# A recurrent scan with a gated feed-forward on one core: parameters transposed behind the dummies, statistics of slab 2 moved from VectorE to ScalarE, and one y moved a gate step

## The chip, the core and the metric

One core of one Trainium2 chip. The metric is the device time of one launch in microseconds (us). Most executions of a kernel agree within 0.3%, and some lie 1 to 2 us higher. TensorE is called PE here, GpSimd is POOL and the DMA-issuing queue is SP, as in the profile.

## The reference, cut to what matters

```python
xn = layernorm(x)                                   # x: 2048 x 512, bf16
Lam_bar = exp(dt * Lam);  Bu = einsum(xn, B_bar)    # complex state of 512
h_t = Lam_bar * h_{t-1} + Bu_t                      # 2048 steps
s = 2 * real(einsum(h, C)) + xn * Dskip
g = silu((gelu(xn @ w_gate) * (xn @ w_up)) @ w_down)   # F = 1376
return x + s * g
```

## The kernel before

The 2048 tokens are worked through in four slabs of 512. For each slab PE computes 11 gate steps (`gate` and `up`, eight matmuls a step), the inputs u of the scan for the slab that follows, the down projection f, and the outputs y of the slab before, four tiles of eight matmuls. VectorE does the complex recurrence in three pieces (rotate, scan, rotate back into `hst`), the products of gate and up, and the epilogue. ScalarE empties PSUM with Gelu, Silu and copies. It also writes a "seed", the skip term, into the PSUM bank of each y before its matmuls accumulate on it. The kernel has eight PSUM buffers of 512 fp32 columns (`bufs=8`), and a gate step takes two of them.

Engines work in program order. Only VectorE's order is computed at build time: `later` puts work in a queue with an estimated cost, and `dve` lets out what fits before a given time.

```python
# the order of a gate step in slab s > 0
if s > 0 and j in Y_AT[s]:
    y_seed(s - 1, Y_AT[s].index(j))          # ScalarE writes the seed
ffn(s, j, ats[s])                            # PE gate, up; ScalarE Gelu, copy; VectorE product
...
    if j in Y_AT[s]:                         # PE: the eight matmuls of y; VectorE: epilogue
        m = Y_AT[s].index(j)
        epi(s - 1, m, y_mm(s - 1, m, hsts[s - 1], y_pss[s - 1, m]), g2s[s - 1, m])
    if s < NS - 1 and XN_AT[s] <= j < XN_AT[s] + M:
        ln_out(s + 1, j - XN_AT[s])          # scale x of the next slab, transpose it by DMA
...
def ln_act(s, m):                            # statistics on ScalarE (before: slab 3 only)
    for i, f in enumerate((AF.Copy, AF.Square)):
        ACT(out=junk[:], in_=x_tok[:, s * M + m, :], func=f, accum_out=sx[:, s, i, m : m + 1])
# end of slab 1: last y of slab 0, and the load of slab 3 behind its output on SP
        if s > 0 and NFT in Y_AT[s]:
            epi(s - 1, M - 1, ...)
        if s == 1:
            load_x(3)
```

Of the kernel before, what the change touches and what calls it, by code (L numbers as in the profile page):

```python
# [19 lines left out]
def kernel(  # L20
# [129 lines left out]
    def dummies(n):  # L150
        w_ps = psum.tile([P, TS], FP32, name="w_ps", tag="ps")
        for _ in range(n):
            nc.tensor.matmul(w_ps[:, :], lhsT=warm[:, 0:P], rhs=warm[:], start=True, stop=True)
# [5 lines left out]
    def bn(s, m):  # L159
        nc.vector.bn_stats(out=st[:, s, m, :], in_=x_tok[:, s * M + m, :])  # L160

    def bn_end(s, m):
        nc.vector.bn_aggr(out=mv[:, s, m, :], in_=st[:, s, m, :])
# [27 lines left out]
    ch = consts.tile(W3, BF16, name="ch")  # L191


    dummies(6)
    pt_ps = psum.tile([P, 16], BF16, name="pt_ps", tag="ps")
    nc.tensor.transpose(pt_ps[:, :], pv[:, :], ident[0:16, 0:16])
    dummies(4)
    def xnT_out(eng, m, tp, k0=0, k1=KT):
        o = xnT[:, k0:k1, m * P : (m + 1) * P]
        if eng is nc.scalar:  # L200
# [1 line left out]
        else:  # L202
            eng.tensor_copy(out=o, in_=tp[:, k0:k1, :])

    ACT(out=pf[:], in_=pt_ps[:, :], func=AF.Copy)
    nc.gpsimd.tensor_tensor(out=dt_[:], in0=euler[:], in1=ldt, op=ALU.pow)
    GT, GS = nc.gpsimd.tensor_tensor, nc.gpsimd.tensor_scalar
# [4 lines left out]
    GT(out=ang[:], in0=ang[:], in1=kr[:], op=ALU.subtract)  # L212
    GT(out=a1[:], in0=lre, in1=dt_[:], op=ALU.mult)
    GT(out=rho[:], in0=euler[:], in1=a1[:], op=ALU.pow)
    for m in range(2):
        bn(0, m)
    bn_end(0, 0)
    bn_end(0, 1)
    rstd0(0, 2)
    xs = [norm0(0), norm0(1)]  # L220
    tps = [t_xn0(0, xs[0]), t_xn0(1, xs[1])]
    xnT_out(nc.vector, 0, tps[0])
# [2 lines left out]
    bn(0, 3)  # L225
    bn_end(0, 2)
    bn_end(0, 3)
    ACT(out=kr[:], in_=ang[:], func=AF.Abs)
    rstd0(2, 4)
    ACT(out=tiny[:], in_=halfpi[:], func=AF.Sin)  # L230
    xs += [norm0(2), norm0(3)]
# [29 lines left out]
        early[3, up] = gu_mm(0, 3, up, 0, TS // 2)  # L261
    xnT_out(nc.vector, 2, tp2[:, 0, :, :])
    ACT(out=sh[:], in_=ang[:], func=AF.Sin, scale=TWO_PI)
    ACT(out=ch[:], in_=kr[:], func=AF.Sin, scale=-TWO_PI, bias=halfpi[:])
    xnT_out(nc.scalar, 3, tp2[:, 1, :, :])


    s2, c2 = (consts.tile([P, NPT, 2], FP32, name=n) for n in ("s2", "c2"))
# [92 lines left out]
    def later(ready, cost, f, key=None):  # L361
        waiting.append((ready, cost, f, key))
# [3 lines left out]
    U_BUFS = 3  # L366
    Z_BUFS = 9
    U0_AT = (5, 7)
    Y_AT = {1: (8, 9, 10, 11), 2: (3, 4, 5, 6), 3: (2, 4, 6, 8)}
    XN_AT = {1: 1, 2: 3}  # L370

    def u_pair(s, h):
        cols = slice(s * TS, (s + 1) * TS)
# [17 lines left out]
    def rotate(dst, src, h, ops, ready, key):  # L391
        hs = slice(h * H2, (h + 1) * H2)
        W = [P, 2, H2, TS]
        box = {}

        def mul(key, tab):
            def f():
                box[key] = work.tile(W, BF16, name=key, tag=key, bufs=1)
                TT(out=box[key][:], in0=src()[:], in1=tab[:, hs, :].unsqueeze(1).to_broadcast(W), op=ALU.mult)  # L399
            return f  # L400

        def comb(i, op):
            return lambda: TT(out=dst()[i], in0=box["pp"][:, i, :, :], in1=box["qq"][:, 1 - i, :, :], op=op)  # L403

        later(ready, 1.17, mul("pp", cos_b), key)
        later(ready, 1.19, mul("qq", sin_b), key)
        for i in range(2):
            later(ready, 0.62, comb(i, ops[i]), key)
# [50 lines left out]
    def ffn(s, j, at):  # L459
        fs = min(P, F - j * P)  # L460
        if s == 0 and j < SPLIT:
            g_ps, u_ps = (gu_mm(s, j, up, TS // 2, TS, early[j, up]) for up in range(2))
        else:
            g_ps, u_ps = gu_mm(s, j, 0), gu_mm(s, j, 1)
        pe_takes(2 * KT)
        i = j % 2
        if i == 0:
            pair["g"] = work.tile([P, 2, TS], BF16, name="gt", tag="gt", bufs=3)
            pair["u"] = work.tile([P, 2, TS], BF16, name="ub", tag="ub", bufs=3)
        gt, ub = pair["g"], pair["u"]  # L470
        ACT(out=gt[:fs, i, :], in_=g_ps[:fs, :], func=AF.Gelu_apprx_tanh)  # L471
        ACT(out=ub[:fs, i, :], in_=u_ps[:fs, :], func=AF.Copy)  # L472
        lag = 1.4
        if s == 0:
            clk["act"] = max(clk["act"], now() - 0.5) + 1.0
            lag = clk["act"] + 0.4 - now()
        if j == NFT - 1:
            dve(now() + lag, 0.36, lambda: TT(out=at[:fs, j, :], in0=gt[:fs, 0, :], in1=ub[:fs, 0, :], op=ALU.mult))  # L478
        elif i:
            dve(now() + lag, 0.63, lambda: TT(out=at[:, j - 1 : j + 1, :], in0=gt[:], in1=ub[:], op=ALU.mult))  # L480

    def down(s, m, at):
        m0 = m * P
# [70 lines left out]
    def ln_small(s):  # L554
        total, var = sx[:, s, 0, :], sx[:, s, 1, :]

        def f():
            STT(out=mq[:, s, :], in0=total, scalar=-1.0 / (D * D), in1=total, op0=ALU.mult, op1=ALU.mult)
            TSC(out=nm[:, s, :], in0=total, scalar1=-1.0 / D, scalar2=None, op0=ALU.mult)
            STT(out=var, in0=var, scalar=1.0 / D, in1=mq[:, s, :], op0=ALU.mult, op1=ALU.add)  # L560
            TSC(out=var, in0=var, scalar1=EPS, scalar2=None, op0=ALU.add)

        dve(now() + 1.0, 0.3, f)
        nc.gpsimd.tensor_tensor(out=rs[:, s, :], in0=var, in1=mhalf[:], op=ALU.pow)
        nc.gpsimd.tensor_tensor(out=nb[:, s, :], in0=nm[:, s, :], in1=rs[:, s, :], op=ALU.mult)


    zs, y_pss = {}, {}
# [10 lines left out]
    def ln_out(s, m):  # L579
        flush(("z", s - 1, m))  # L580
        xn = work.tile([P, D], BF16, name="xn", tag="xn", bufs=4)
        ACT(out=xn[:], in_=x_tok[:, s * M + m, :], func=AF.Identity, scale=rs[:, s, m : m + 1], bias=nb[:, s, m : m + 1])
        xn_out(s, m, xn)

    def xn_out(s, m, xn):
# [19 lines left out]
    def ln_vector_small(x):  # L605
        G.tensor_scalar(out=vx[:, x, :], in0=mv[:, x, :, 1], scalar1=EPS, scalar2=None, op0=ALU.add)
        G.tensor_tensor(out=rs[:, x, :], in0=vx[:, x, :], in1=mhalf[:], op=ALU.pow)
        G.tensor_tensor(out=nb[:, x, :], in0=mv[:, x, :, 0], in1=rs[:, x, :], op=ALU.mult)
        G.tensor_scalar(out=nb[:, x, :], in0=nb[:, x, :], scalar1=-1.0, scalar2=None, op0=ALU.mult)

    vx = consts.tile([P, NS, M], FP32, name="vx")
    ln_vector(1)
    ln_vector_small(1)
    later(13.0, 1.25, lambda: TT(out=v4(t2_[:]), in0=v4(sa[:]), in1=sB, op=ALU.mult))
    for m in range(M):
        skip(0, m, xs[m])
    xs1 = {}
# [12 lines left out]
    for s in range(NS):  # L630
        for j in range(NFT):
            if s > 0 and j in Y_AT[s]:
                y_seed(s - 1, Y_AT[s].index(j))
            ffn(s, j, ats[s])
            if s == 0:
                if j == 1:
                    coefficients()
                if j in U0_AT:
                    chain(0, U0_AT.index(j), u_pair(0, U0_AT.index(j)), hst0)
                if j == 5:  # L640
                    for m in range(M):
                        later(0.0, 0.72, lambda m=m: (bn(2, m), bn_end(2, m)), "n")
                if j == NFT - 1:
                    flush("n")
                    ln_vector_small(2)
                if j == 8:
                    coefficients_end()
                if 3 <= j < 3 + M:
                    flush(("xn", j - 3))
                    xn_out(1, j - 3, xs1[j - 3])  # L650
                if j == 2 + M:
                    load_c(0)
                    nc.sync.dma_start(
                        out=wd[:, 0 : NFT - 1, :],
                        in_=B_w_down[0 : (NFT - 1) * P, :].rearrange("(k p) d -> p k d", p=P),
                    )
                    nc.sync.dma_start(out=wd[:FL, NFT - 1, :], in_=B_w_down[(NFT - 1) * P : F, :])
                    load_c(1)
            else:
                if j in Y_AT[s]:  # L660
                    m = Y_AT[s].index(j)
                    epi(s - 1, m, y_mm(s - 1, m, hsts[s - 1], y_pss[s - 1, m]), g2s[s - 1, m])
                if s < NS - 1 and XN_AT[s] <= j < XN_AT[s] + M:
                    ln_out(s + 1, j - XN_AT[s])
        if s < NS - 1:
            hsts[s + 1] = work.tile([P, 2, NPT, TS], BF16, name="hst", tag="hst")
            ats[s + 1] = work.tile([P, NFT, TS], BF16, name="at", tag="at")
            for h in range(2):
                chain(s + 1, h, u_pair(s + 1, h), hsts[s + 1])
                if h == 0 and s > 0 and NFT in Y_AT[s]:  # L670
                    y_seed(s - 1, M - 1)
            if s > 0 and NFT in Y_AT[s]:
                epi(s - 1, M - 1, y_mm(s - 1, M - 1, hsts[s - 1], y_pss[s - 1, M - 1]), g2s[s - 1, M - 1])
            if s == 1:
                load_x(3)
            for m in range(M):
                g2s[s, m] = down(s, m, ats[s])
                if s == 0:
                    fold_c(m)
                if s == 1:  # L680
                    ln_act(3, m)
            if s == 1:
                ln_small(3)
# [42 lines left out]
```

## Time and profile before

| | before |
|---|---|
| median of 4 runs | 185.35 us (185.21 to 185.49) |
| profiled span | 183.7 us |
| PE / VectorE / ScalarE / POOL busy | 96% / 87% / 64% / 15% |
| first matmul of slab 1 / 2 / 3 | 51.48 / 93.80 / 137.41 us |
| first matmul of the last, halved y | 178.23 us |

The start times of the slabs are the rulers of this document: PE is nearly always busy, so a wait added or removed shows as a shift of the next slab's start. The prediction shows the page's first row, PE's waits and the timeline, and reads them.

### The profile page before, as it was taken

The page shows a single profiled execution, that of the slowest core. Times are in us where ns is not written, and L with a number is a line of the kernel's source. Part 1 is how long each engine was busy: PE and PEld are TensorE (multiplying, and loading weights), DVE is VectorE, ACT ScalarE, POOL GpSimd, SP SyncE. Part 2 cuts the span into 40 slices and gives each one's busy share as a digit, 9 for nine tenths or more (in the row PEclk, how much of TensorE's full clock was granted, in tenths as well). Part 3 has the DMA queues.
Part 4 walks back from the last instruction along what each step waited for, and adds up shares of the span by engine and source line. Part 5 has one row for each costly group of instructions (what it writes and reads, how often), then busy time and mean ns, then how long its engine had stood idle before and what let it go on. Part 6 is the DMA issues. An engine that isn't in the chain of part 4 may idle for free.

```text
span 183.7 us, 2426 instructions
## 1 busy us (share of the span) xinstructions
PE 175.4 (96%) x840; PEld 84.1 (46%) x855; DVE 160.4 (87%) x251; ACT 116.9 (64%) x207; POOL 27.2 (15%) x50
## 2 busy tenths in 40 slices
PE   6989999999999999999999799999999999999992
PEld 1676444444444444444444344444444444444451
DVE  3579999899999899899958999999999999996063
ACT  3299766768789974474499875667529445574510
POOL 3879917000700000000004000000000000000000
PEclk9999999999999999999999999999999999999999
DMA  5999595790001300100400023300000000000012
GB/s 148 311 362 150 109 235 105 207 249 0 0 0 29 79 10 29 42 15 29 114 4 0 0 57 86 87 5 0 0 0 0 0 30 32 29 29 0 0 48 66
DMA packets 25643, 12.37 MB, mean 67 GB/s; under 512 B 15808, under 2 KB 25632, under 8 KB 25632
## 3 DMA queue, kind: packets, MB, share of 16 engines
q1 hardware_dynamic: 25456, 12.16, 27.7%
q8 instruction: 6, 0.10, 0.2%
q10 hardware_dynamic: 176, 0.07, 0.1%
q14 instruction: 5, 0.04, 0.1%
HBM read 6.46 MB, written 2.10 MB: 47 GB/s over the span
## 4 chain that ended last, share of the span: by engine, by line
PE 73%; DVE 9%; ACT 8%; DMA 3%; issue 2%; POOL 2%; ACTq 1%; SPq 0%; DVEq 0%; POOLq 0%
PE up_ps L243 17%; PE g_ps L243 17%; PE f_ps L487 14%; PE y_ps L507 13%; PE u_ps L382 11%; DVE Ft L429 3%; ACT junk L552 2%; DMA x_tok<-in_A_x_dram 2%; DVE yg L520 2%; DMA pv<-in_A_Dskip_dram 1%; DVE pp L399 1%; ACT gt L471 1%; ACT ub L472 1%; ACT g L492 1%; DVE ot L521 1%
## 5 line engine op out<-in xcount | busy, mean ns | idle before, releaser
L243 PE MATMUL up_ps<-xnT,wu 128*128 128x512 bf16 (+2 forms) x188 | 45.2, 361 | 0.9 <-ACT xnT L201 0.7
L243 PE MATMUL g_ps<-xnT,wg 128*128 128x512 bf16 (+3 forms) x193 | 45.5, 357 | 0.4 <-ACT xnT L201 0.2
L487 PE MATMUL f_ps<-wd,at 128*128 128x512 bf16 (+1 forms) x172 | 38.7, 379 | 0.3
L471 ACT ACTIVATE gt<-g_ps 128x512 bf16<-128x512 f32 (+1 forms) x44 | 26.8, 608 | 17.0 <-PE g_ps L243 15.3
L472 ACT ACTIVATE ub<-up_ps 128x512 bf16<-128x512 f32 (+1 forms) x44 | 26.9, 612 | 6.7 <-PE up_ps L243 5.8
L429 DVE TENSOR_TENSOR_SCAN Ft<-rho,it,Wt 128x512 bf16<-128x512 f32 x24 | 29.3, 1266 | 0.0
L507 PE MATMUL y_ps<-C,hst 128*128 128x512 bf16 x120 | 28.0, 379 | 1.2 <-ACT y_ps L499 1.1
L382 PE MATMUL u_ps<-xnT,BT 128*128 128x512 bf16 x124 | 28.2, 379 | 0.2
L243 PEld LDWEIGHTS <-wu 128*128 128x128 bf16 (+1 forms) x192 | 19.2, 100 | 19.7 <-issue 0.9
L243 PEld LDWEIGHTS <-wg 128*128 128x128 bf16 (+1 forms) x196 | 19.3, 100 | 19.2 <-issue 0.6
L487 PEld LDWEIGHTS <-at 128*128 128x128 bf16 (+1 forms) x176 | 17.1, 98 | 21.1 <-DVE at L478 0.5
L387 ACT ACTIVATE U<-u_ps 128x512 bf16<-128x512 f32 x32 | 19.0, 597 | 9.8 <-PE u_ps L382 9.4
L382 PEld LDWEIGHTS <-BT 128*128 128x128 bf16 x128 | 12.5, 98 | 15.0
L492 ACT ACTIVATE g<-f_ps 128x512 f32<-128x512 f32 x16 | 9.5, 594 | 15.2 <-PE f_ps L487 15.2
L507 PEld LDWEIGHTS <-hst 128*128 128x128 bf16 x120 | 11.7, 98 | 15.4 <-issue 1.4
L520 DVE TENSOR_TENSOR yg<-y_ps,g 128x512 bf16<-128x512 f32 x15 | 10.2, 683 | 9.1 <-PE y_ps L507 9.0
L480 DVE TENSOR_TENSOR at<-gt,ub 128x1024 bf16<-128x1024 bf16 x20 | 13.6, 681 | 1.6 <-ACT ub L472 1.5
L403 DVE TENSOR_TENSOR hst<-pp,qq 128x1024 bf16<-128x1024 bf16 x16 | 10.4, 688 | 0.3
L403 DVE TENSOR_TENSOR Wt<-pp,qq 128x1024 bf16<-128x1024 bf16 x16 | 10.4, 687 | 0.2
L399 DVE TENSOR_TENSOR pp<-U,cos_b 128x2048 bf16<-128x2048 bf16 x8 | 9.7, 1218 | 0.0
L399 DVE TENSOR_TENSOR qq<-U,sin_b 128x2048 bf16<-128x2048 bf16 x8 | 9.7, 1217 | 0.0
L399 DVE TENSOR_TENSOR pp<-Ft,cos_b 128x2048 bf16<-128x2048 bf16 x8 | 9.7, 1216 | 0.0
(108 smaller groups left out, 153.9 us busy)
## 6 DMA issues: line engine op xcount, KB each, us to landing
out_dram<-ot SPq DMA_DIRECT2D x15, 128.0 KB, 1.7
x_tok<-in_A_x_dram SPq DMA_DIRECT2D x3, 512.0 KB, 6.8
wd<-in_B_w_down_dram SPq DMA_DIRECT2D x1, 1280.0 KB
wg<-in_B_w_gate_dram SPq DMA_DIRECT2D x2, 256.0 KB, 4.3
wu<-in_B_w_up_dram SPq DMA_DIRECT2D x2, 256.0 KB
wg<-in_B_w_gate_dram SPq DMA_DIRECT2D x1, 512.0 KB, 6.5
wu<-in_B_w_up_dram SPq DMA_DIRECT2D x1, 512.0 KB
wg<-in_B_w_gate_dram SPq DMA_DIRECT2D x1, 352.0 KB
```

The source lines that it names most:

```text
L243: nc.tensor.matmul(ps[:fs, a:b], lhsT=w[:, kt, fsl], rhs=xnT[:, kt, s * TS + a : s * TS + b], start=(kt == 0), stop=(kt == KT - 1),)
L382: nc.tensor.matmul(u_ps[:, :], lhsT=BT[:, ri, kt, pt * P : (pt + 1) * P], rhs=xnT[:, kt, cols], start=(kt == 0), stop=(kt == KT - 1),)
L387: ACT(out=U[:, ri, q, :], in_=u_ps[:, :], func=AF.Copy)
L399: TT(out=box[key][:], in0=src()[:], in1=tab[:, hs, :].unsqueeze(1).to_broadcast(W), op=ALU.mult)
L403: return lambda: TT(out=dst()[i], in0=box["pp"][:, i, :, :], in1=box["qq"][:, 1 - i, :, :], op=op)
L429: nc.vector.tensor_tensor_scan(out=box["F"][:, ri, q, :], data0=rho[:, pt : pt + 1].to_broadcast([P, TS]), data1=box["W"][:, ri, q, :], in ...
L471: ACT(out=gt[:fs, i, :], in_=g_ps[:fs, :], func=AF.Gelu_apprx_tanh)
L472: ACT(out=ub[:fs, i, :], in_=u_ps[:fs, :], func=AF.Copy)
L480: dve(now() + lag, 0.63, lambda: TT(out=at[:, j - 1 : j + 1, :], in0=gt[:], in1=ub[:], op=ALU.mult))
L487: nc.tensor.matmul(f_ps[:, :], lhsT=at[:fs, k, m0 : m0 + P], rhs=wd[:fs, k, :], start=(k == 0), stop=(k == NFT - 1))
L507: nc.tensor.matmul(y_ps[:, :], lhsT=hst[:, j // NPT, j % NPT, m0 : m0 + P], rhs=C2[:, j // NPT, j % NPT, :], start=False, stop=(j == 2 * N ...
L520: TT(out=yg[:], in0=y_ps[:, :], in1=g2[:], op=ALU.mult)
```

## The change

The intent has three parts. The head should no longer make the first x tiles queue behind the parameters. VectorE should lose the statistics of slab 2, which ScalarE takes up in slab 1. The y of slab 1 should come one gate step later, where PE waited for its seed.

```diff
-    dummies(6)
+    dummies(8)
     nc.tensor.transpose(pt_ps[:, :], pv[:, :], ident[0:16, 0:16])
-    dummies(4)
+    dummies(1)
+    for m in range(2):                  # moved up from behind the POOL block
+        bn(0, m)
+    ... bn_end(0, 0); bn_end(0, 1); rstd0(0, 2)
     ACT(out=pf[:], in_=pt_ps[:, :], func=AF.Copy)
 ...                                     # Abs now stands behind the first Sin,
 ...                                     # the copy of x tile 3 ahead of the second Sin
-    Y_AT = {1: (8, 9, 10, 11), 2: (3, 4, 5, 6), 3: (2, 4, 6, 8)}
-    XN_AT = {1: 1, 2: 3}
+    Y_AT = {1: (8, 9, 10, 11), 2: (4, 5, 6, 7), 3: (2, 4, 6, 8)}
+    XN_AT = {1: 7, 2: 3}
+    ST_AT = (0, 1, 2, 4)
 ...                                     # queue costs: 1.17 -> 1.19, 0.63 -> 0.65, one 1.25 -> 2.0
     def ln_out(s, m):
-        ACT(out=xn[:], in_=x_tok[...], func=AF.Identity, scale=rs[...], bias=nb[...])
+        if s == NS - 1: ...the same on ScalarE...
+        else:
+            dve(now() + 1.0, 0.36, lambda: TSC(out=xn[:], in0=x_tok[...], ..., op0=ALU.add, op1=ALU.mult))
 ...
-                if j == 5:              # slab 0: statistics of slab 2 on VectorE
-                    for m in range(M):
-                        later(0.0, 0.72, lambda m=m: (bn(2, m), bn_end(2, m)), "n")
+                if s == 1 and j in ST_AT:
+                    ln_act(2, ST_AT.index(j))
+                    if j == ST_AT[-1]:
+                        ln_small(2)
+                if s == 1 and j in (XN_AT[1], XN_AT[1] + 1):
+                    for m in (2 * (j - XN_AT[1]), 2 * (j - XN_AT[1]) + 1):
+                        ln_out(2, m)
```

More of the change, by code (lines that the diff above doesn't have):

```diff
@@ L203, in xnT_out @@
             eng.tensor_copy(out=o, in_=tp[:, k0:k1, :])
+    for m in range(2):
+        bn(0, m)
+    bn_end(0, 0)
+    bn_end(0, 1)
+    rstd0(0, 2)
     ACT(out=pf[:], in_=pt_ps[:, :], func=AF.Copy)
@@ L214 @@
     GT(out=rho[:], in0=euler[:], in1=a1[:], op=ALU.pow)
-    for m in range(2):
-        bn(0, m)
-    bn_end(0, 0)
-    bn_end(0, 1)
-    rstd0(0, 2)
     xs = [norm0(0), norm0(1)]
@@ L227 @@
     bn_end(0, 3)
-    ACT(out=kr[:], in_=ang[:], func=AF.Abs)
     rstd0(2, 4)
@@ L263 @@
     ACT(out=sh[:], in_=ang[:], func=AF.Sin, scale=TWO_PI)
+    ACT(out=kr[:], in_=ang[:], func=AF.Abs)
+    xnT_out(nc.scalar, 3, tp2[:, 1, :, :])
     ACT(out=ch[:], in_=kr[:], func=AF.Sin, scale=-TWO_PI, bias=halfpi[:])
-    xnT_out(nc.scalar, 3, tp2[:, 1, :, :])
     s2, c2 = (consts.tile([P, NPT, 2], FP32, name=n) for n in ("s2", "c2"))
@@ L403, in comb @@
             return lambda: TT(out=dst()[i], in0=box["pp"][:, i, :, :], in1=box["qq"][:, 1 - i, :, :], op=op)
-        later(ready, 1.17, mul("pp", cos_b), key)
+        later(ready, 1.19, mul("pp", cos_b), key)
         later(ready, 1.19, mul("qq", sin_b), key)
@@ L479, in ffn @@
         elif i:
-            dve(now() + lag, 0.63, lambda: TT(out=at[:, j - 1 : j + 1, :], in0=gt[:], in1=ub[:], op=ALU.mult))
+            dve(now() + lag, 0.65, lambda: TT(out=at[:, j - 1 : j + 1, :], in0=gt[:], in1=ub[:], op=ALU.mult))
     def down(s, m, at):
@@ L564, in ln_small @@
         nc.gpsimd.tensor_tensor(out=rs[:, s, :], in0=var, in1=mhalf[:], op=ALU.pow)
-        nc.gpsimd.tensor_tensor(out=nb[:, s, :], in0=nm[:, s, :], in1=rs[:, s, :], op=ALU.mult)
+        if s == NS - 1:
+            nc.gpsimd.tensor_tensor(out=nb[:, s, :], in0=nm[:, s, :], in1=rs[:, s, :], op=ALU.mult)
     zs, y_pss = {}, {}
@@ L581, in ln_out @@
         xn = work.tile([P, D], BF16, name="xn", tag="xn", bufs=4)
-        ACT(out=xn[:], in_=x_tok[:, s * M + m, :], func=AF.Identity, scale=rs[:, s, m : m + 1], bias=nb[:, s, m : m + 1])
+        if s == NS - 1:
+            ACT(out=xn[:], in_=x_tok[:, s * M + m, :], func=AF.Identity, scale=rs[:, s, m : m + 1], bias=nb[:, s, m : m + 1])
+        else:
+            dve(now() + 1.0, 0.36, lambda: TSC(
+                out=xn[:], in0=x_tok[:, s * M + m, :], scalar1=nm[:, s, m : m + 1], scalar2=rs[:, s, m : m + 1],
+                op0=ALU.add, op1=ALU.mult,
+            ))
         xn_out(s, m, xn)
@@ L607, in ln_vector_small @@
         G.tensor_tensor(out=rs[:, x, :], in0=vx[:, x, :], in1=mhalf[:], op=ALU.pow)
-        G.tensor_tensor(out=nb[:, x, :], in0=mv[:, x, :, 0], in1=rs[:, x, :], op=ALU.mult)
-        G.tensor_scalar(out=nb[:, x, :], in0=nb[:, x, :], scalar1=-1.0, scalar2=None, op0=ALU.mult)
     vx = consts.tile([P, NS, M], FP32, name="vx")
@@ L613 @@
     ln_vector_small(1)
-    later(13.0, 1.25, lambda: TT(out=v4(t2_[:]), in0=v4(sa[:]), in1=sB, op=ALU.mult))
+    later(13.0, 2.0, lambda: TT(out=v4(t2_[:]), in0=v4(sa[:]), in1=sB, op=ALU.mult))
     for m in range(M):
@@ L639 @@
                     chain(0, U0_AT.index(j), u_pair(0, U0_AT.index(j)), hst0)
-                if j == 5:
-                    for m in range(M):
-                        later(0.0, 0.72, lambda m=m: (bn(2, m), bn_end(2, m)), "n")
-                if j == NFT - 1:
-                    flush("n")
-                    ln_vector_small(2)
                 if j == 8:
@@ L662 @@
                     epi(s - 1, m, y_mm(s - 1, m, hsts[s - 1], y_pss[s - 1, m]), g2s[s - 1, m])
-                if s < NS - 1 and XN_AT[s] <= j < XN_AT[s] + M:
-                    ln_out(s + 1, j - XN_AT[s])
+                if s == 1 and j in ST_AT:
[5 more added lines that the diff above has]
+                        ln_out(2, m)
+                if s == 2 and XN_AT[2] <= j < XN_AT[2] + M:
+                    ln_out(3, j - XN_AT[2])
         if s < NS - 1:
```

## The prediction

> **What bounds the kernel now.** I read the busy shares first, then the list of waits for the matmul engine, then the timeline where those waits fall.
>
> ```profile
> PE 175.4 (96%) x840; PEld 84.1 (46%) x855; DVE 160.4 (87%) x251; ACT 116.9 (64%) x207; POOL 27.2 (15%) x50
> ...
> PE w_ps L153 <- DVE halfpi L126: 1.2, 1, 1.2
> PE y_ps L507 <- ACT y_ps L499: 1.1, 1, 1.1
> PE up_ps L243 <- ACT xnT L201: 0.7, 1, 0.7
> PE pt_ps L196 <- DMA pv<-in_A_Dskip_dram: 0.5, 1, 0.5
> PE g_ps L243 <- ACT xnT L201: 0.2, 1, 0.2
> ```
>
> PE is busy 175.4 of 183.7 us. It idles 3.7 us in these five waits and about 3.5 us in the tail, where the last results are multiplied and stored. So a change pays only if it shortens the head or removes the wait of 1.1 us at 102 us, and it costs what it adds in new PE waits. VectorE (87%) and ScalarE (64%) matter only where PE waits for them in program order. The head, in the timeline:
>
> ```profile
> 4.45 0.17 PE L196 MATMUL pt_ps<-ident,pv 16*128 16x16 bf16 x1 [0.54 <-DMA pv<-in_A_Dskip_dram]
> ...
> 6.23 1.06 PE L181 MATMUL tp<-ident,xn 128*128 128x128 bf16 x8
> ...
> 8.91 0.37 ACT L228 ACTIVATE kr<-ang 128x196 f32<-128x196 f32 x1 [0.99 <-POOL ang L212]
> ...
> 12.13 0.60 PE L243 MATMUL up_ps<-xnT,wu 128*128 128x256 bf16 x4 [0.71 <-ACT xnT L201]
> ```
>
> The parameters' transpose waits for its DMA, four dummies queue behind it until 6.23, and the first x tiles (ready at about 5.65) queue behind those. ScalarE holds the second deviation behind an Abs that waits for GpSimd. Slab 1 starts at 51.5:
>
> ```profile
> 53.51 1.28 ACT L471 ACT_TABLE_LOAD   x1
> 54.80 0.60 ACT L471 ACTIVATE gt<-g_ps 128x512 bf16<-128x512 f32 x1
> ...
> 56.73 0.83 ACT L582 ACTIVATE xn<-x_tok,nb,rs 128x512 bf16<-128x512 bf16 x1
> ...
> 65.98 0.60 ACT L499 ACTIVATE y_ps<-x_tok 128x512 f32<-128x512 bf16 x1
> ...
> 67.02 1.89 PE L507 MATMUL y_ps<-C,hst 128*128 128x512 bf16 x8
> ```
>
> ScalarE starts the first Gelu 2.2 us after its matmul ended, works without a pause and has caught up by 65. The seed of the first y starts at 65.98, just in time for PE at 67.02. This is the place to watch.
>
> **What the Trainium skill says.** "TensorE: Matmul & The Clock Gate", Part 1, says the array runs at half clock until about 3.4 us of sustained activity; the trace agrees (dummies start every 0.427 us, later matmuls of the same width every 0.216), so the dummies buy the clock. The same page, Architectural detail, calls ScalarE and VectorE strict FIFO; the Abs above, holding a ready square root, agrees. "ScalarE: Activation LUTs", What ACT_TABLE_LOAD costs, gives about 1283 ns; the trace shows 1.28 us. Its Table sets section says cheap functions sit in every set. Copy and Square run here between Silus without a load; between Gelus no run shows it yet, I assume the same. "VectorE: DVE Perf Modes" (Mode 4x) lets a one-source bf16 operation run faster than a two-source one: the scaling line starts every 0.36 us for 512 elements, the two-source product takes 0.60 for 1024.
>
> **The change part by part.**
> Head. Eight dummies end at 1.17 + 8 x 0.427 = 4.59; the parameters have landed at 4.32, so the 0.54 wait goes; one dummy ends at 5.1. The first deviation no longer stands behind the parameters' copy: 4.45 instead of 4.74. x tile 0 is then ready at 5.35 and transposed at about 5.6 instead of 6.23: 0.6 us. The copies and the first gate groups follow 0.6 earlier (weights had landed at 5.5, 6.6, 7.5 and 8.6 by the landing times in the trace, so they don't stop it). The second square root goes from 9.18 to about 8.15, Sin's table load from 9.48 to 8.45. The transposes of tiles 2 and 3 come at 9.75 (10.38), ScalarE copies tile 3 at 10.4 (11.49), and the group that waits for that PSUM buffer starts at 11.05 instead of 12.13. **Head: 1.05 us gained**, and nothing before 51 us seems to take it back.
>
> VectorE. Four statistics with aggregation, 42.66 to 45.87, go: -3.2 us. Added in slab 1: four scalings at 0.36 and the four small operations, about 2.0 us. That is off the path unless VectorE waits in order.
>
> ScalarE in slab 1. Four scalings of 0.70 go (-2.8). Added before y are four pairs of Copy and Square with accumulator reads. Such a pair takes 1.37 us in slab 2 (91.94 to 93.31): +5.5 us, all in gate steps 0, 1, 2 and 4. Gelu and copy start every 0.476 us when back to back. From the first Gelu to the first seed are now 16 x 0.476 + 4 x 1.37 = 13.1 us, and PE starts y 0.72 after the seed began (101.28 to 102.00): 13.8 us. PE gets to this y 67.02 - 54.80 = 12.2 us after the first Gelu. **New wait: 1.6 us.** With 8 PSUM banks PE can be four gate steps ahead, so I see none before it.
>
> VectorE in order behind this. I stepped through the program's queue bookkeeping (it gives the order of the trace before exactly). The products of gate and up wait for ScalarE: pair 0-1 at 57.2, pair 2-3 at 61.9, the small operations until 64.4. The saved 3.2 us are spent waiting, the last rotation before y ends at about 67.5, as late as the seed. Then the two scalings, the other half of the rotation and the first epilogue push the last two scalings to 72.1. Their transposing DMAs stand behind the first output on the queue: 72.9 and 74.2 plus 2.6 us to land = 76.8. PE would reach u of slab 2, which needs them, at 67.57 + 8.63 = 76.2: **another 0.6 us**. The last epilogue of slab 0 ends near 87.2 (85.7 before), and the load of slab 3 is issued behind it.
>
> The later y. That load gates the statistics of slab 3 on ScalarE, without a pause from 90.1 to 104:
>
> ```profile
> 90.08 0.63 ACT L552 ACTIVATE junk<-x_tok 128x512 bf16<-128x512 bf16 x1 [2.62 <-DMA x_tok<-in_A_x_dram]
> ...
> 101.28 0.66 ACT L499 ACTIVATE y_ps<-z 128x512 f32<-128x512 bf16 x1
> ...
> 102.00 1.89 PE L507 MATMUL y_ps<-C,hst 128*128 128x512 bf16 x8 [1.13 <-ACT y_ps L499]
> ```
>
> One gate step of 1.73 us ahead of y looks like it buries the 1.13. But the seed now also stands behind Gelu and copy of that step (0.96) and the first scaling of slab 3 (0.70), which kept its place: 1.66 us. Alone, the move gains under 0.1 us. With the chain 1.5 later: first Gelu 99.9, seed 104.4, y 105.15, against 102.00 + 1.73: PE is 1.4 us behind the kernel before. VectorE, full from 97.4 to 160, is behind by the same.
>
> Sum: head -1.05, seed wait +1.6, late transpose +0.6, slab 2 about +0.2 to +0.3: **about +1.4 us, 186.7**.
>
> **Rivals.** (a) The head's gain holds and the waits of slab 1 do not come, for instance because ScalarE's pairs are shorter or PE waits earlier and harmlessly: 185.3 - 1.05 = 184.3, with the y move fully effective 183.2. For it: VectorE loses work and the constants look tuned. Against: the sum of 13.8 against 12.2 us uses only durations in the trace. (b) VectorE becomes the bound from 97 us on and the delay grows: its order is nearly unchanged there and its work is equal, so not over +2: 187.5. (c) The clock gate opens a window later because there are nine dummies and a gap: some 3 us of matmuls at half speed, +1.6 us. Gaps were as long before, so unlikely. (d) Square forces table loads between Gelus: 8 x 1.28 us on ScalarE, over 190. Very unlikely.
>
> **Range and chances.** I trust the waits more than rival (a), but their sizes hang together, so I put the time a little below the sum: 186.4, with 184.2 to 187.6 for eight in ten. Two per cent are 3.7 us: faster would need more than all PE waits that the change touches, 0.02; slower needs (d) or several added waits, 0.04; same 0.94.
>
> **What would show it.** Right: tile transposes at about 5.6, the group behind tile 3's copy near 11; y of slab 0 waiting for the ScalarE seed by 1 to 2 us near 66; VectorE idle before gate products at 55 to 62; u of slab 2 waiting for transposing DMAs by about half a microsecond; y of slab 1 still waiting for its seed. Wrong: y at 66 starting without a wait, Copy and Square shorter than 1.3 us a pair, slab 3's load issued earlier than 86 us, or a PE stall inside the gate steps for lack of PSUM.

## The result, and the profile after

The changed kernel takes 186.42 us (median of 4 runs, 186.27 to 186.45) against 185.35. The ratio is 1.0056, with a 95% interval of 1.0039 to 1.0074. Ratios are the mean time of one kernel's fast runs over that of the other's in the same rounds, so they are not quite the ratio of the medians. The change is small, and it is a loss.

The first row of the page of the changed kernel, and its list of PE's waits (engine, tile and line, whom it waited for: us in total, times, longest):

```profile
PE 175.2 (95%) x839; PEld 83.8 (45%) x854; DVE 159.4 (86%) x251; ACT 118.8 (64%) x219; POOL 26.1 (14%) x45
```

PE does the same work and the other engines are no fuller. The waits tell more:

```profile
PE y_ps L508 <- DVE hst L404: 1.5, 1, 1.5
PE w_ps L153 <- DVE halfpi L126: 1.2, 1, 1.2
PE up_ps L242 <- ACT xnT L201: 0.7, 1, 0.7
PE y_ps L508 <- ACT y_ps L500: 0.6, 1, 0.6
PE u_ps L383 <- DMA xnT<-xn: 0.5, 1, 0.5
PE g_ps L242 <- DVE xnT L203: 0.2, 1, 0.2
```

The wait for the parameters' DMA is gone. Two waits are new: y of slab 0 (1.5 us, put down to VectorE's rotation), and u of slab 2 on the transposing DMA (0.5). The wait of the y of slab 1 for its seed has shrunk from 1.1 to 0.6. The timeline of the head after (start, length, engine, line, operation):

```profile
5.49 0.92 PE L181 MATMUL tp<-ident,xn 128*128 128x128 bf16 x8
...
10.14 0.42 DVE L203 COPY xnT<-tp 128x512 bf16<-128x512 bf16 x1 [0.49 <-PE tp L181]
...
10.60 0.60 ACT L201 ACTIVATE xnT<-tp 128x512 bf16<-128x512 bf16 x1 [0.28 <-DVE xnT L203]
...
11.25 0.60 PE L242 MATMUL up_ps<-xnT,wu 128*128 128x256 bf16 x4 [0.71 <-ACT xnT L201]
```

The group that waits for tile 3's copy starts at 11.25 instead of 12.13. Slab 1 of the changed kernel, in the same view:

```profile
53.91 0.60 ACT L472 ACTIVATE gt<-g_ps 128x512 bf16<-128x512 f32 x1
...
57.37 0.69 DVE L481 TENSOR_TENSOR at<-gt,ub 128x1024 bf16<-128x1024 bf16 x1 [1.68 <-ACT ub L473]
...
67.11 0.64 ACT L500 ACTIVATE y_ps<-x_tok 128x512 f32<-128x512 bf16 x1
67.11 0.68 DVE L404 TENSOR_TENSOR hst<-pp,qq 128x1024 bf16<-128x1024 bf16 x1
...
67.80 1.89 PE L508 MATMUL y_ps<-C,hst 128*128 128x512 bf16 x8 [1.51 <-DVE hst L404]
...
77.13 7.07 PE L383 MATMUL u_ps<-xnT,BT 128*128 128x512 bf16 x31 [0.54 <-DMA xnT<-xn]
```

ScalarE's seed and VectorE's last rotation both start at 67.11. The profile puts the wait down to the one that came last, and here that misleads. All eight matmuls of y need the seed, but by the loop in `y_mm` only the last two need the last of the four pieces in which the rotation writes `hst`. So the seed held the start; the run with the first seed earlier, below, shows the difference. VectorE sat idle 1.68 us at 57.37 for a product whose `up` ScalarE had not copied yet.

| first matmul of | before | after | shift |
|---|---|---|---|
| slab 1 gates | 51.48 | 50.59 | -0.89 |
| slab 2 gates | 93.80 | 95.28 | +1.48 |
| slab 3 gates | 137.41 | 138.38 | +0.97 |
| the last, halved y | 178.23 | 178.97 | +0.74 |

The head gains 0.89 us, and slab 1 loses 2.37 of PE time. By the starts of the matmuls this is all at two places: y comes 17.21 us after the start of slab 1 instead of 15.54 (1.67), and u 9.33 us after y instead of 8.63 (0.70). The waits in the list are shorter because they count from the modelled end of the matmul before. Slab 2 gives back 0.51, and slab 3 and the final part another 0.23. The profiled span grew by 0.7 us and the median by 1.07. The profiled execution of the kernel before took 185.93 us, 0.58 over its median, and that of the changed kernel 186.43; one profile of each cannot say where the 0.58 lies, so the shifts above are good to about half a microsecond in sum.

### The profile page after: what moved, and what is told of

The parts are those of the page before. It is cut to its first block, busy times and chain, and to the rows that moved or that the text cites. A ratio compares the mean times of both kernels' runs of the same rounds, so it can differ in the third digit from the quotient of the medians.

```text
span 184.4 us, 2433 instructions
## 1 busy us (share of the span) xinstructions
PE 175.2 (95%) x839; PEld 83.8 (45%) x854; DVE 159.4 (86%) x251; ACT 118.8 (64%) x219; POOL 26.1 (14%) x45
## 4 chain that ended last, share of the span: by engine, by line
PE 64%; DVE 14%; ACT 14%; issue 3%; DMA 3%; SPq 0%; DVEq 0%; ACTq 0%
PE f_ps L488 15%; PE up_ps L242 13%; PE g_ps L242 13%; PE u_ps L383 11%; PE y_ps L508 10%; ACT junk L553 5%; DMA x_tok<-in_A_x_dram 3%; DVE Ft L430 3%; ACT ub L473 2%; ACT gt L472 2%; DVE qq L400 2%; DVE yg L521 2%; ACT L472 1%; DVE hst L404 1%; DVE at L481 1%
## 5 line engine op out<-in xcount | busy, mean ns | idle before, releaser
L565 POOL TENSOR_TENSOR rs<-sx,mhalf 128x4 f32<-128x4 f32 x2 | 3.7, 1860 | 65.5 <-ACT gt L472 33.6
L553 ACT ACTIVATE junk<-x_tok 128x512 bf16<-128x512 bf16 x16 | 10.1, 629 | 2.4 <-DMA x_tok<-in_A_x_dram 2.2
L404 DVE TENSOR_TENSOR Wt<-pp,qq 128x1024 bf16<-128x1024 bf16 x16 | 10.4, 686 | 0.2
```

Of the source, the lines that this page charges most:

```text
L404: return lambda: TT(out=dst()[i], in0=box["pp"][:, i, :, :], in1=box["qq"][:, 1 - i, :, :], op=op)
```

## The experiments

All outputs are right. Each time stands beside runs of the kernel before on the same chip, whose median differed by session (185.92, 185.85 and 185.49 us), so kernels of different sessions are compared by ratio. The intervals are about 0.3 to 0.6 per cent wide to each side, so most single steps are read from the traces. This table has the length of each stretch in us, from the first gate matmul of one slab to that of the next, and from slab 3 to the last, halved y:

| | slab 1 | slab 2 | slab 3 to the halved y |
|---|---|---|---|
| before | 42.32 | 43.61 | 40.82 |
| changed | 44.69 | 43.10 | 40.59 |
| head alone | 42.32 | 43.66 | 40.82 |
| statistics and scaling alone | 44.68 | 43.77 | 40.59 |
| y later, alone | 42.33 | 43.64 | 40.82 |
| y later, scalings later | 42.32 | 47.05 | 40.82 |
| changed, first seed earlier | 45.22 | 43.68 | 40.59 |
| changed, products later | 44.01 | 43.53 | 40.59 |
| changed, both | 44.48 | 43.39 | 40.59 |
| changed, scalings first | 44.17 | 44.30 | 40.60 |
| changed, load earlier | 44.66 | 42.63 | 40.59 |
| head, y later, its first seed not | 42.33 | 42.32 | 41.28 |
| head, load earlier | 42.32 | 42.47 | 40.82 |
| head, all of these | 42.32 | 42.32 | 40.82 |

**Head alone** (on the kernel before): the first half of the diff above, down to the copies of the x tiles, and nothing else.

> The head alone on the kernel before (dummies 8 and 1, statistics ahead of the parameters' copy, Abs later). The changed kernel starts slab 1 0.89 us earlier (50.59 against 51.48). My theory: nothing behind the head gives it back, every later wait hangs on that start, so 185.35 - 0.89 = 184.5 us and the y of slab 1 still waits 1.1 us. Rival (VectorE or a load fixes a later time): part of it is lost at the load of slab 3 or at the last products, 184.9 to 185.3.

Measured: 185.19 us, ratio 0.9946 (0.9918 to 0.9975). The y of slab 1 still waits 1.2 us for its seed. Ratio 0.9946 of 185.35 is a gain of 1.0 us, and the later stretches are as long as before: the head's gain reaches the end.

**Statistics and scaling alone** (on the kernel before, with the queue costs):

```diff
+    ...statistics of slab 2 by ln_act in slab 1, scaling on VectorE, XN_AT[1] = 7
     Y_AT = {1: (8, 9, 10, 11), 2: (3, 4, 5, 6), 3: (2, 4, 6, 8)}   # as before; old head
```

> Only the statistics and scaling of slab 2 (with the queue costs that came with them), old head, y of slab 1 at its old steps. My theory: the first y of slab 0 waits about 1.5 us, u of slab 2 about 0.5 us for the transposing DMAs, and the y of slab 1 starts some 1.9 us later than before: 187.3 us. Rival (the loss comes from the later y or from the changed head, and the move is paid for by the 3.2 us that VectorE saves): 185.4 or less, no wait at the first y of slab 0.

Measured: 187.93 us, ratio 1.0107 (1.0076 to 1.0137), a loss of 2.0 us. PE's waits in it, from the same list:

```profile
PE y_ps L508 <- DVE hst L404: 1.5, 1, 1.5
PE y_ps L508 <- ACT y_ps L500: 1.3, 1, 1.3
...
PE u_ps L383 <- DMA xnT<-xn: 0.5, 1, 0.5
```

The whole loss lies in this part, and its slab 1 is as long as that of the changed kernel. The rival, which had VectorE's saved time paying for it, falls.

**y a step later, alone**: `2: (3, 4, 5, 6)` to `2: (4, 5, 6, 7)` on the kernel before.

> Only the y of slab 1 a gate step later, rest as before. My theory: the seed stands behind Gelu and copy of that step and the first scaling of slab 3 (1.66 us), so the first y starts at about 103.7 where before it would stand at 102.0 + 1.73: 185.3 us, a wait of about 1.1 us stays. Rival (the gate step buries the wait): 184.3.

Measured: 185.81 us, ratio 1.0001 (0.9968 to 1.0035), and the wait is still 1.2 us. Its three stretches sum to 126.79 us, those of the kernel before to 126.75. The gate step buries nothing, because the seed moved with it. The three parts add up: -0.54% + 1.07% + 0.01% = +0.54%, where the change as a whole measured +0.56%; each part is known to about 0.3 points.

**y a step later, scalings of slab 3 two steps later**: also `XN_AT = {1: 1, 2: 5}`.

> The y move with the scalings of slab 3 two steps later, so that the seed stands behind Gelu and copy alone. My theory: seed at 102.25, y at 102.95, PE ready at 102.45: the wait falls to about 0.5 and 0.75 us are gained: 184.6. Rival (VectorE is full from 97 to 160 us and sets the end): the wait falls to 0.5 all the same, but the time stays at 185.2 to 185.4 and PE waits for the last products or the last rotation instead.

Measured: 189.22 us, ratio 1.0157. The seed's wait fell to 0.5 and y began at 102.94, as computed, but there is another wait, which I had not looked for:

```profile
122.76 2.74 PE L382 MATMUL u_ps<-xnT,BT 128*128 128x512 bf16 x6 [2.40 <-DMA xnT<-xn]
```

The scalings' transposing DMAs now stand on SP behind the outputs of four epilogues, and u of slab 3 waits for the last of them. The last scaling also comes late on ScalarE itself (117.44), and the run does not part the two. After the wait the matmuls start every 0.43 us instead of 0.22 until about 126 us, at a granted clock of 0.50 in the trace: u takes 8.4 us to the next group instead of 6.9. So slab 2 loses 2.6 us by the wait and 1.5 by the clock, less 0.6 won at the seed. Four of the six executions had a mean granted clock of 0.991 like this one and took 189.2 to 189.7 us; the two at 1.000 took 188.2 and 188.5. So it does not answer whether VectorE ties with PE. A later run asks that again.

**First seed earlier** (on the changed kernel): the ScalarE seed of slab 0's first y is issued ahead of the Gelu of step 3 instead of step 8.

```diff
-            if s > 0 and j in Y_AT[s]:
+            if s > 0 and (j in Y_AT[s][1:] or j == (3 if s == 1 else Y_AT[s][0])):
...                                         # the tile's number in the next line to match
```

> The changed kernel with the first seed of slab 0 issued before the Gelu of gate step 3 instead of step 8, nothing else. In the changed kernel seed (67.7) and the last rotation on VectorE (67.8) are ready at the same time, while PE could start y at 66.25. My theory (both hold it): the early seed pushes the later statistics by 0.5 us, the rotation ends half a microsecond later, y starts at about 68.2, time 186.4 to 186.9 on the scale of 186.42. Rival (the seed alone holds it): the wait of 1.5 us goes, 184.9.

Measured: 187.44 us, ratio 1.0077 (1.003 to 1.0124). The timeline of PE and VectorE:

```profile
66.15 0.59 PE L508 MATMUL y_ps<-C,hst 128*128 128x512 bf16 x2
...
66.17 0.69 DVE L404 TENSOR_TENSOR hst<-pp,qq 128x1024 bf16<-128x1024 bf16 x1
...
66.92 1.04 PE L508 MATMUL y_ps<-C,hst 128*128 128x512 bf16 x4 [0.18 <-DVE hst L404]
...
67.39 0.69 DVE L404 TENSOR_TENSOR hst<-pp,qq 128x1024 bf16<-128x1024 bf16 x1
...
68.13 0.60 PE L508 MATMUL y_ps<-C,hst 128*128 128x512 bf16 x2 [0.17 <-DVE hst L404]
...
77.41 7.07 PE L383 MATMUL u_ps<-xnT,BT 128*128 128x512 bf16 x32 [1.77 <-DMA xnT<-xn]
```

I had expected y to start whole, at 68.2. Instead its first two matmuls started at 66.15 and the rest followed as pieces of `hst` came, the last pair at 68.13: y ended about 1 us earlier than in the changed kernel. So the rotation without the seed delays PE by 0.98 us of the 1.67 (the gate step after y starts 18.24 us into the slab, 18.94 in the changed kernel, 17.26 before). Of the 0.98, 0.54 come from the edit itself: the early seed pushes the last piece of the rotation back from 16.52 to 17.06 us into the slab. My estimate is that the rotation alone would have cost the changed kernel about 0.4 us (0.98 - 0.54). None of the second was won, since u of slab 2 started at 77.41 (77.13 in the changed kernel) with a wait of 1.77 for the DMA. The DMA hangs on the statistics, which the early seed had pushed back. Slab 1 is 0.53 us longer than in the changed kernel, and slab 2 another 0.58: the y of slab 1 now waits 1.2 us for its seed.

**Gate products later in VectorE's order** (on the changed kernel):

```diff
-        lag = 1.4
+        lag = 4.4 if s == 1 and j < 6 else 1.4
```

> The changed kernel with the gate products of steps 0 to 5 of slab 1 put 3 us later in VectorE's order, so that VectorE does scans and rotation instead of waiting for ScalarE. My theory (both hold it): the rotation ends near 65.5, y still starts at 67.8, now behind ScalarE's seed: wait 1.5 us, time within 0.3 of the changed kernel. Rival (VectorE's order alone holds it): the wait goes, 184.9.

Measured: 186.43 us, ratio 1.0032 (0.9974 to 1.009). The wait of y stays 1.5 us and its releaser is now ScalarE's seed, although VectorE started the last piece of the rotation at 66.49, 2.5 us before the seed began at 68.95:

```profile
69.65 1.89 PE L508 MATMUL y_ps<-C,hst 128*128 128x512 bf16 x8 [1.53 <-ACT y_ps L500]
```

So the seed by itself keeps the whole wait, and the rotation, in the run above, a part of it. The DMA wait at u is gone here, and slab 1 is 0.68 us shorter than in the changed kernel; slab 2 gives 0.43 of it back, with 1.1 us of waiting for the seed of its y. All times in this trace are later by about 2 us for another reason, told at the end.

**Both edits together.**

> Both edits. My theory: y starts at 66.3 with a wait under 0.3 us, but the scalings keep their place, so the transposing DMAs of slab 2 land only near 76.5 where PE is ready at 74.9: the wait there grows from 0.5 to about 1.6 us and the gain is 0.6: about 185.8. Rival (the wait at y is the whole loss): 184.9.

Measured: 186.46 us, ratio 1.0026 (0.9982 to 1.007). The wait at y is gone, and y starts at 66.37. The DMA takes nearly all of it:

```profile
76.87 7.07 PE L383 MATMUL u_ps<-xnT,BT 128*128 128x512 bf16 x32 [1.71 <-DMA xnT<-xn]
```

So slab 1 is held by a chain, not by one wait: ScalarE's statistics, VectorE's small operations, POOL's power, VectorE's scalings, two pairs of DMA transposes, u. Remove the wait at y and PE merely arrives earlier at the end of that chain: slab 1 is only 0.21 us shorter than in the changed kernel, and slab 2 is 0.29 longer, where the seed wait of its y is 0.9. The interval of this ratio overlaps that of the changed kernel, so the verdict rests on the two waits and not on the time; the gain of 0.6 that I expected does not show.

**All four scalings ahead of the first epilogue** (on the changed kernel):

```diff
-                if s == 1 and j in (XN_AT[1], XN_AT[1] + 1):
-                    for m in (2 * (j - XN_AT[1]), 2 * (j - XN_AT[1]) + 1):
+                if s == 1 and j == XN_AT[1]:
+                    for m in range(M):
```

> The changed kernel with all four scalings of slab 2 ahead of the first epilogue. My theory: the transposing DMAs land 0.6 us earlier and the wait of 0.54 us at u goes, but the load of slab 3 hangs on VectorE's last epilogue, which does not move, so the wait at the y of slab 1 grows from 0.6 to about 1.1 us: 186.3 to 186.4. Rival (waits add up): 185.9.

Measured: 187.09 us, ratio 1.0056 (1.0018 to 1.0095), the ratio of the changed kernel itself. The DMA wait is gone, and the seed's wait in slab 2 has grown from 0.6 to 1.8:

```profile
105.38 1.89 PE L508 MATMUL y_ps<-C,hst 128*128 128x512 bf16 x8 [1.82 <-ACT y_ps L500]
```

The growth of 1.2 has three terms. PE starts slab 2 0.52 us earlier, the load of slab 3 is issued 0.16 later (87.93), and it took 3.85 us to the first statistics (91.78), where in the profile of the changed kernel it took 3.34. The last term I had not expected.

**The load of slab 3 earlier** (on the changed kernel): `load_x(3)` on SP ahead of the last output of slab 0.

```diff
+            if s == 1:
+                load_x(3)
             if s > 0 and NFT in Y_AT[s]:
                 epi(s - 1, M - 1, ...)
-            if s == 1:
-                load_x(3)
```

> The changed kernel with the load of slab 3 ahead of the last output of slab 0. In the changed kernel the load is issued at 87.8 us, 1.6 us later than before, and I take the 0.6 us wait at the y of slab 1 to hang on it. My theory: the wait goes, ratio 1.0056 - 0.0033 = about 1.0025. Rival (VectorE's backlog from slab 1 sets the end by itself): the wait goes, ratio stays at 1.005.

Measured: 186.02 us, ratio 1.002 (0.9991 to 1.0049). The load is issued at 81.93 instead of 87.77, and the seed's wait in slab 2 is no longer in PE's list. The point estimate is the expected one. Its interval is too wide to exclude the rival by time, but the trace speaks against it: slab 2 is 0.47 us shorter than in the changed kernel, and the stretch behind it is no longer (40.59 in both).

**Three candidates on the head alone.** First, y of slab 1 a step later with its first seed left at step 3 (so seed and y no longer move together):

> Head alone plus the y of slab 1 a gate step later, with its first seed left where it was (ahead of Gelu of step 3). The head alone measured 0.9946 of the kernel before. If PE alone sets the end: the wait of 1.2 us at the y of slab 1 goes and 1.1 us are gained on top: ratio 0.9885. If VectorE, full from 97 us to the end, ties with PE: the wait goes but the time stays near the head alone: 0.993 to 0.995, with a new wait for VectorE near the last products.

Measured: 184.46 us, ratio 0.9961 (0.9917 to 1.0004); four executions of six lie at 184.18 to 184.52, two at 186.1, at a granted clock of 0.991 instead of 0.999 to 1.000. No wait at the y of slab 1 is left. Part of that may be the load of slab 3, which took 3.39 us here and 3.94 in the head alone. A wait at the end has taken part of its place:

```profile
PE f_ps L487 <- DVE at L478: 0.5, 1, 0.5
```

From the start of slab 3 to the halved y this kernel needs 176.49 - 135.21 = 41.28 us, the head alone 177.56 - 136.74 = 40.82: VectorE takes back 0.46. This is the tie that the fourth run had failed to show; the interval of the ratio is too wide to show it by time. In this kernel VectorE still waits, in order, for the statistics of slab 3 before it goes on.

Second, the head and the earlier load of slab 3, on the head alone:

> Head alone plus the load of slab 3 issued ahead of the last output of slab 0 instead of behind it: one line moved. Then ScalarE starts the statistics of slab 3 some 2.5 us earlier and its first Gelu of slab 2 about 1.1 us earlier, and VectorE's small operations on them also. Both theories (PE alone, or PE tied with VectorE) expect 1.0 us on top of the head: ratio 0.989.

Measured: 183.94 us, ratio 0.9907 (0.9877 to 0.9938). Here ScalarE and VectorE come forward too, no wait at y is listed, and slab 3 to the halved y is 177.86 - 137.04 = 40.82 us again. (The profile caught its slowest execution, 185.60 us; the others took 183.73 to 184.13.)

Third, both, with VectorE's small operations later as well:

> Both of these and the small operations of slab 3's statistics one rotation step later on VectorE. There is one PE wait of 1.2 us to take away, so no more than 1.2 us over the head alone: ratio 0.988 to 0.989 if VectorE does not bind; if VectorE binds at the end this one should be the fastest of the three.

Measured: 183.90 us, ratio 0.9911 (0.9882 to 0.9939), the same as the second. **The head with one line moved beats both kernels**: 1.5 us under the kernel before in the same rounds, by the medians, where the change lost 1.0.

## Why the prediction was right

The time, 186.4 for 186.42, the direction and the mechanism were right. The agreement to 0.02 us is partly luck: the sum of the steps was 186.7, and I put the figure lower in favour of rival (a).

- **Head.** Said 1.05, measured 0.89 in the trace and 1.0 in time, and it reaches the end. The missing 0.16 has mostly one term: I let ScalarE copy tile 3 at 10.4, and it waited for VectorE's copy of tile 2 until 10.60. Both tiles lie in one PSUM bank. The Trainium skill, "PSUM — Partial Sum Buffer", PSUM bank collisions, says that two engines on one bank and quadrant must be kept apart; the trace of the changed kernel agrees, since it names VectorE's copy as what ScalarE waited for (0.28 us), and ScalarE starts 0.04 us after that copy's end. The copies of tiles 0 and 1, which have a buffer each, overlap by 0.11 us (VectorE 6.13 to 6.55, ScalarE from 6.44). No run puts tiles 2 and 3 into two banks. I had the page and did not apply it.
- **The seed.** Said 1.6; measured 1.67 by the starts of the matmuls (1.5 in the list). The sum of ScalarE's work carried it: first Gelu to y took 13.89 us. That the rotation would be ready "as late as the seed" was exact in time, but it weighs less than that sounds: y starts without its last piece. The runs with one edit each show that the seed alone keeps the whole delay and the rotation alone 0.98 us, of which the edit made 0.54.
- **The transposing DMAs.** Said 0.6, measured 0.70 by the starts (0.54 in the list). The forecast that they would absorb a gain at y held too (1.71 us in the run with both edits).
- **The later y.** Said to gain under 0.1 alone, measured ratio 1.0001, and 0.04 us lost in the trace.
- **Slab 2 and the end: the mis-sized term.** I expected 0.2 to 0.3 more loss there, with y of slab 1 at 105.15; it came at 104.69, and the trace shows 0.51 and 0.23 given back. The first is the load of slab 3, which took 3.34 us in this profile and 3.89 in the one of the kernel before. I do not know why: among the eleven profiled runs with the load in its old place, nine took 3.8 to 4.0 and two 3.3 to 3.4, one of those with slab 1 unedited. The second goes with a side effect that I had not sized. In the changed kernel the last gate product stands ahead of VectorE's rotation (165.16, just behind 164.46; before, the rotation's product at 164.08 came between), and PE's wait inside the down projection vanished (9.67 us for the group instead of 9.90). The same order shows in the runs that carry the new queue costs, and not in the head alone. That the costs do it is read from the orders and not tested alone.
- **Rivals.** (a) fell with the wait at y. (b) fell for the changed kernel, whose last stretch is 0.23 us shorter than before; VectorE comes near it, as the first candidate shows, where it takes back 0.46 us once PE's wait in slab 2 is removed. (c) occurs, but with the old head too (below): in one of four profiles, and in two of ten with the new head, which is too few to compare. (d) fell: between the Gelus of slab 1 no table load stands.
- **Two readings that went too far.** In the section on the Trainium skill the traces show the two rates of the clock, but not the 3.4 us: the first eight transposes of x, 5.1 us after the first dummy, still take 1.06 us where eight later ones take 0.61 (6.23 and 10.38 in the kernel before). And 0.36 us for 512 elements against 0.60 for 1024 does not show a faster one-source operation: that is 0.70 ns per element against 0.59. Only the measured durations entered the sum.

## What to carry to other kernels

Work moved to an engine with a low average share is not free: add up what that engine must do in order between the event that starts it and the event that the critical engine waits for, and compare it with the time the critical engine needs for the same stretch. Before removing a wait, look for the next thing at the end of the same chain, here a DMA queue in program order. An operation that stands behind another on a queue only because it was written later, such as the load of slab 3 behind an output, can be worth more than moving work: one line gave 0.7 us over the head alone by the two ratios (0.9946 and 0.9907 of 185.35, whose intervals overlap) and 1.19 by the table, and the whole change lost 1.0.

## What the Trainium skill lacked or had wrong

- "ScalarE: Activation LUTs", Table sets: names copy, identity and abs as filler of every set, but not Square. The eight Copy and Square operations of slab 1 in the changed kernel stand between Gelus without a load.
- The same page, What ACT_TABLE_LOAD costs: 1283 ns for the load agrees (1.28 us), but the total of about 2.66 us per switch does not show here. The load at 52.62 is followed by the Gelu at 53.91, 1.29 us for the switch.
- "ScalarE: Activation LUTs" gives no price for the accumulator output. Here every use adds a separate 0.19 us read, and a Copy and Square pair with two reads takes 1.37 us where two plain 512-column operations take 0.95.
- "TensorE: Matmul & The Clock Gate" calls the moment of opening run-variable and counts it under 1% of a span, which holds, but a comparison within 1% is of that size. In the profile of the run with later gate products the first 256-column group of `up` took 1.91 us:

```profile
8.58 1.91 PE L242 MATMUL up_ps<-xnT,wu 128*128 128x256 bf16 x8
```

  The same group takes 1.04 in the changed kernel; that execution took 187.88 us where others of the same kernel took 185.81 to 186.45. The profile of the run with y alone moved shows it too (1.56; 187.31 against 185.65 to 186.83), with the old head, and so does that of the head with the earlier load (1.60; 185.60 against 183.73 to 184.13).
- No page gives the time of a small transposing DMA from SBUF to SBUF as this kernel sees it ("DMA: Bandwidth & Descriptors" has only the sequencer's cycles for 8,192 tiles, without the transfer): about 1.25 us of the queue for each, in order, and 2.6 us from issue to the matmul that needs it (second of the pair issued at about 74.5, u at 77.13).
